# A batch's first 128 channels on all partitions for the first two steps, and half of K's weight loads moved behind V's

## The chip, the cores and the metric

The kernel runs on one core of a Trainium2 chip. The metric is device microseconds of one execution; the time before is 411.26 us, the median of three runs (411.04 to 411.67). The engines are named as in the profile: PE is the matrix engine (PEld its weight loads), ACT the scalar engine, DVE the vector engine, POOL the engine that issues the loads which convert float32 to bfloat16, SP the engine that issues the other transfers.

## What is computed

```python
# x: 8 batches x 4160 positions x 192 channels, float32; 8 heads of 24 channels, 7 taps
w = softmax(weight, axis=-1)                      # 8 x 7
y[b, t, h, g] = sum_k w[h, k] * x[b, t - 6 + k, h, g]      # causal convolution
xk = mu_k * y + (1 - mu_k) * y_prev               # y_prev: y of the position before
xr = mu_r * y + (1 - mu_r) * y_prev
k = relu(xk @ w_k)                                # 192 -> 1024
v = (k * k) @ w_v                                 # 1024 -> 192
out = sigmoid(xr @ w_r) * v                       # w_r: 192 -> 192
```

## The kernel before

Two batches are worked on as a pair, four pairs one after the other. What PE multiplies by the weights has the channels on the partitions. The 192 channels of a batch are three thirds of 64, and a plane `c` of `yT`, `xk` or `xr` holds third `c` of the pair's first batch on partitions 0 to 63 and the same third of its second batch on 64 to 127. So every product with `w_k` or `w_r` is a matmul of 64 rows, and two of them, one for each batch, run side by side in the two halves of the array (the profile shows them as `64*128`). Both halves need the weights, so `w_k` and `w_r` are loaded twice, once for partitions 0 to 63 and once for 64 to 127.

A pair is cut into steps of 512 positions; the first pair begins with one of 256. A step has slots: a slot (`k_mm`, L591) fills one PSUM tile of 128 x 1024 in six or twelve matmuls, ACT takes it out with a Relu (`k_relu`, L603), DVE squares it (`k_square`, L617). Step 0 has four slots (numbers 0 to 3), step 1 eight (4 to 11). `r` (L648) makes the gate's PSUM tile, `v_rows` (L679) multiplies the squares by `w_v`, `v_out` (L695) multiplies by the gate and sends the result out. The ring of PSUM tiles has four places, which K, the convolution, R and V share.

The order of all engines is written out by hand. `prologue` loads and prepares; `bundle_first` convolves the first two groups of positions, 3 and 4 blocks of 120 (`conv_t`, L411: matmuls of 128 rows by 32, 24, 16 or 8 columns, four at a time; `to_yT`, L421, casts the result into `yT`), and runs slots 0 to 3; `bundle_second` has slots 4 to 7, with the third group's convolution between them and a convolution in another form at its end (`conv_mm`, L391); `bundle_third` has slots 8 to 11 with R and V of step 0 between; `bundle_rest` is all the rest, and begins step 2 with slot 12. It transposes a group of convolved rows (`tr`, L500) and convolves group 4, loaded as the last thing of `prologue`, with `conv_tiles` (L317).

POOL's queue holds the converting loads in the order of `prologue`: group 1 of x, the first half of the columns of `w_k` (`load_wk`, two loads, L224), the second half (two), groups 2 and 3 of x, `w_r` (two), `w_v`, group 4 of x (four). Group 0 of x comes as float32 from the queues of ACT and SP, and ACT casts it; behind it SP loads the two rows of mixing factors (`load_mu`), which PE turns in one small matmul (`turn_mu`, L280).

Of the kernel before, what the change touches and what calls it, by code (L numbers as in the profile page):

```python
# [14 lines left out]
def kernel(  # L15
# [11 lines left out]
    nc = tc.nc  # L27
# [22 lines left out]
    SHORT = 78  # L50
    FILL = (6, 3)

    const = ctx.enter_context(tc.tile_pool(name="const", bufs=1))
# [10 lines left out]
    for p in range(NPAIR):  # L64
# [5 lines left out]
        for L in sizes:  # L70
# [3 lines left out]
            t0 += L  # L74
    T0, LAST = S - TAIL, len(steps) - 1
    NSLOT = len(slots)

# [96 lines left out]
    def load_mu(i, m):  # L174
# [3 lines left out]
        )  # L178

    place = three.tile([P, NF * STEP], FP32, tag="k2", name="x_f32")  # L180
    n = groups[0][2] * 2 * D
# [12 lines left out]
    tap8 = const.tile([8, P + 8], BF16)  # L194
    ident6 = const.tile([2 * NC, 2 * NC], FP32)
    ones6 = const.tile([2 * NC, 2 * NC], FP32)
    mu_raw = const.tile([2 * NC, P], FP32)
    warm_ps = ring.tile([P, 2, BANK], FP32, tag="k", name="warm")
# [3 lines left out]
    toe = const.tile([P, H, P], BF16)  # L202
    mu = const.tile([P, 2, NC], FP32)

# [5 lines left out]

    def load_thirds(w, m, n, cs=slice(0, NC)):
        for st in range(2):
            nc.gpsimd.dma_start(
                out=w[st * Q : (st + 1) * Q, cs, :],
                in_=bass.AP(
                    tensor=m.tensor,
                    offset=m.offset + cs.start * Q * n,
                    ap=[[n, Q], [Q * n, cs.stop - cs.start], [1, n]],
                ),
            )  # L220

    def load_wk(c0, c1):
        for st in range(2):
            nc.gpsimd.dma_start(  # L224
                out=wk[st * Q : (st + 1) * Q, :, c0:c1],
                in_=bass.AP(
                    tensor=moe_w_k.tensor,
                    offset=moe_w_k.offset + c0,
                    ap=[[DF, Q], [Q * DF, NC], [1, c1 - c0]],
                ),  # L230
            )

    def load_wr():
        load_thirds(wr, moe_w_r, D)

# [3 lines left out]
    def softmax():  # L239
        nc.vector.tensor_reduce(out=w_max, in_=w_raw, axis=mybir.AxisListType.X, op=ALU.max, negate=True)  # L240
        nc.scalar.activation(out=w_exp, in_=w_raw, func=AF.Exp, bias=w_max, accum_out=w_sum)
        nc.scalar.preload_act_table(AF.Sigmoid)
        for c in range(NC):
            cs = slice(c * Q, (c + 1) * Q)
            nc.scalar.copy(out=xbs[0][:, :, :, cs], in_=x_f32[:, :, :, cs])
# [33 lines left out]
    def turn_mu():  # L279
        nc.tensor.transpose(out=warm_ps[:, 1, 0 : 2 * NC], in_=mu_raw, identity=ident6)  # L280

# [119 lines left out]
    def conv_t(g, c, o, blocks):  # L401

        for n, i in enumerate(blocks):
            for first_piece in (True, False):
                for s in range(2):
                    for q in range(2):
                        c0 = c * Q + q * 32
                        lo, hi = c0 // G, (c0 + 31) // G
                        h, m = (hi, 32) if first_piece else (lo, hi * G - c0)
                        p0 = s * Q + q * 32  # L410
                        nc.tensor.matmul(  # L411
                            out=o[p0 : p0 + m, n * BLK : (n + 1) * BLK],
                            lhsT=xbs[g][:, i, s, c0 : c0 + m],
                            rhs=toe[:, h, 0:BLK],
                            start=True,
                            stop=True,
                        )

    def to_yT(g, c, o, b0, b1, copy):
        c0 = YC + groups[g][1] + b0 * BLK  # L420
        copy(out=yTs[0][:, c, c0 : c0 + (b1 - b0) * BLK], in_=o[:, 0 : (b1 - b0) * BLK])  # L421

# [27 lines left out]
    def new_yT(p):  # L450
        yTs[p] = two.tile([P, 3, -(-(YC + S) // 16) * 16], BF16, tag="yT", name="yT")
        y_drams[p] = dram.tile([NROW, 2 * D], BF16, tag=f"y{p % 2}", name="y_dram")
        nc.vector.memset(yTs[p][:, :, 0:YC], 0.0)

# [65 lines left out]
    def y_of(s, cs, k):  # L520

        p, t0, L, _, _ = steps[s]
        if s == LAST:
            return y_tail[:, cs, :, k : k + TAIL, :].rearrange("p c a t b -> p c a (t b)")
        return yTs[p][:, cs, YC + t0 - 1 + k : YC + t0 - 1 + k + L]

# [3 lines left out]
    def diff(s, cs=slice(0, 3)):  # L530
        L = steps[s][2]
        if cs.start == 0:
            diffs[s] = three.tile([P, 3, STEP], BF16, tag="diff", name="d")
        nc.vector.tensor_tensor(  # L534
            out=shaped(s, diffs[s][:, cs, :L]), in0=y_of(s, cs, 1), in1=y_of(s, cs, 0), op=ALU.subtract
        )

    def mix(s, i, sl=slice(0, NC)):

        L = steps[s][2]  # L540
        d = diffs[s]
        if s == 0 and i == 0:
            if sl.start == 0:
                xks[s] = two.tile([P, NC, STEP], BF16, tag="xk", name="xk")
            t = xks[s]
            c = sl.start
            nc.vector.scalar_tensor_tensor(
                out=t[:, c, :L],
                in0=d[:, c, :L],
                scalar=mu[:, i, c : c + 1],  # L550
                in1=y_of(s, sl, 0)[:, 0, :],
                op0=ALU.mult,
                op1=ALU.add,
            )
            return
        scale(s, i, *range(sl.start, sl.stop))
        add_y(s, i, sl)

    def scale(s, i, *cs):
        L = steps[s][2]  # L560
        if s not in (xks, xrs)[i]:
            (xks, xrs)[i][s] = (two, three)[i].tile([P, NC, STEP], BF16, tag=("xk", "xr")[i], name=("xk", "xr")[i])
        t = (xks, xrs)[i][s]
        for c in cs:
            nc.vector.tensor_scalar(  # L565
                out=t[:, c, :L], in0=diffs[s][:, c, :L], scalar1=mu[:, i, c : c + 1], scalar2=None, op0=ALU.mult
            )
# [7 lines left out]
    def k_mm(n, cs=range(NC)):  # L575
# [9 lines left out]

        for c in cs:
            for f in range(nf):
                fs = slice((j * nf + f) * P, (j * nf + f + 1) * P)
                for i in range(2):
                    r = slice(i * Q, (i + 1) * Q)  # L590
                    nc.tensor.matmul(  # L591
                        out=ps[:, i, f * L : (f + 1) * L],
                        lhsT=wk[r, c, fs],
                        rhs=xk[r, c, :L],
                        start=c == 0 and f == 0,
                        stop=c == NC - 1 and f == nf - 1,
                    )
# [42 lines left out]
    def r(s, j):  # L640
        xr = xrs[s]
        ps = ring.tile([P, 2, BANK], FP32, tag="k", name="ps_r")
        for k in range(2):
            ts = slice((2 * j + k) * P, (2 * j + k + 1) * P)
            for c in range(NC):
                for i in range(2):
                    q = slice(i * Q, (i + 1) * Q)
                    nc.tensor.matmul(  # L648
                        out=ps[:, i, k * D : (k + 1) * D],
                        lhsT=xr[q, c, ts],  # L650
                        rhs=wr[q, c, :],
                        start=c == 0,
# [170 lines left out]
    def prologue():  # L823
# [10 lines left out]
        load_mu(0, moe_mu_k)  # L834
        load_mu(1, moe_mu_r)
        nc.scalar.preload_act_table(AF.Exp)
        nc.vector.memset(zeros, 0.0)
# [5 lines left out]
        masks_tap()  # L843
        select_equal(ident6, 2 * NC)
        masks_band()
# [19 lines left out]
        load_wr()  # L865
        load_wv()
        x_tile(4)
        load_x(4)

    def bundle_first(ns):  # L870
        new_yT(0)
        tiles = [ring.tile([P, 2, BANK], FP32, tag="k", name="ps_t") for _ in range(2)]
        for n, (g, c) in enumerate((g, c) for g in range(2) for c in range(NC)):
            o = tiles[n % 2][:, n // 2 % 2, :]
            conv_t(g, c, o, range(groups[g][2]))
            if n == 0:
                turn_mu()
            to_yT(g, c, o, 0, groups[g][2], nc.scalar.copy)
            if g == 0:
                diff(0, slice(c, c + 1))  # L880
                if c == 0:
                    nc.vector.tensor_copy(out=mu.rearrange("p i c -> p (i c)"), in_=warm_ps[:, 1, 0 : 2 * NC])
                mix(0, 0, slice(c, c + 1))
# [16 lines left out]
    def bundle_second(b, ns):  # L900
# [7 lines left out]
        outs = [tiles[0][:, 0, :], tiles[1][:, 0, :], tiles[0][:, 1, :]]  # L908
        conv_t(g, 0, outs[0], range(4))
        to_yT(g, 0, outs[0], 0, 4, dve_)  # L910
        k_relu(ns[1])
        conv_t(g, 1, outs[1], range(4))
        to_yT(g, 1, outs[1], 0, 4, dve_)
        k_mm(ns[2])
        k_relu(ns[2])
        conv_t(g, 2, outs[2], range(4))
        to_yT(g, 2, outs[2], 0, 4, act_)
        k_mm(ns[3])
# [146 lines left out]
```

## Time and profile before

| | |
|---|---|
| runs, median | 411.26 us (411.04 to 411.67) |
| the profiled execution, span from its first to its last instruction | 409.5 us |
| its granted PE clock from 7.6 us on | 1.0 |
| PE busy | 401.2 us (98%) |
| DVE busy | 370.4 us (90%) |
| ACT busy | 354.6 us (87%) |
| K matmuls (L591), R (L648), V (L679) | 1632, 780, 4032 |
| converting loads (q0) | 16.36 MB |

The profile gives no time of its execution but the span; the median of the runs lies 1.8 us above it, and that much is taken as what lies around the span. Times in the views are microseconds from the first instruction. A row of the timeline merges neighbours of a kind: start, time until the last one's end, engine, line, operation, output and inputs, shape, count. A matmul's own time is longer than its turn: the next one starts while it still runs, so paces are taken from start to start.

### The profile page before, as it was taken

The numbers are of one execution on the slowest core, as the hardware profiler recorded it, in microseconds if no ns is written. First come the engines' busy times: TensorE is split into PE (matmuls) and PEld (weight loads), VectorE is DVE, ScalarE is ACT, GpSimd is POOL, SyncE is SP. The second block draws the span as 40 slices with busy tenths as digits, with TensorE's granted clock in tenths as the row PEclk, the third lists the DMA queues.
The fourth block names the chain that finished last, engine by engine and source line by source line (L and its number), as shares of the span: only waits on it lengthen the run. The fifth ranks groups of instructions, "written<-read, shape, count | busy, mean of one in ns | idle before, by whom it ended". The sixth has DMA issues, their size and how long they took to land.

```text
span 409.5 us, 17547 instructions
## 1 busy us (share of the span) xinstructions
PE 401.2 (98%) x7736; PEld 302.2 (74%) x7736; DVE 370.4 (90%) x672; ACT 354.6 (87%) x426; POOL 56.8 (14%) x91
## 2 busy tenths in 40 slices
PE   8899999999999999999999999999999999999996
PEld 5567777777877767777776777777777778777795
DVE  5999898988999989999999999999999899999973
ACT  6899989989888989988898998889899878877781
POOL 8622202200230202004020022000000000000000
PEclk9999999999999999999999999999999999999999
DMA  9999999997399998789995996977623856221223
GB/s 148 188 201 207 197 204 192 213 249 179 90 203 264 193 193 134 158 212 178 205 141 151 236 170 132 171 176 206 121 91 89 209 135 157 80 71 48 80 80 115
DMA packets 138955, 66.23 MB, mean 162 GB/s; under 512 B 89356, under 2 KB 138880, under 8 KB 138880
## 3 DMA queue, kind: packets, MB, share of 16 engines
q1 hardware_dynamic: 95536, 48.20, 46.9%
q0 software_dynamic: 42544, 16.36, 34.8%
q8 instruction: 60, 0.98, 0.9%
q10 hardware_dynamic: 800, 0.57, 0.5%
q14 instruction: 15, 0.12, 0.1%
HBM read 33.29 MB, written 36.86 MB: 171 GB/s over the span
## 4 chain that ended last, share of the span: by engine, by line
PE 92%; DMA 4%; POOL 1%; DVE 1%; ACT 1%; issue 1%; POOLq 0%; DVEq 0%
PE ps_v L679 41%; PE ps_k L591 39%; PE ps_r L648 8%; PE ps_c L362 2%; DMA xb<-in_x_dram 2%; DMA wk<-in_moe_w_k_dram 2%; PE ps_v L631 1%; ACT k_sb L603 1%; PE ps_c L317 0%; POOL wk L224 0%; POOL xb L152 0%; DVE k L617 0%; DVE yT L421 0%; DVE o_sb L695 0%; POOL tap L258 0%
## 5 line engine op out<-in xcount | busy, mean ns | idle before, releaser
L603 ACT ACTIVATE k_sb<-ps_k 128x1024 bf16<-128x1024 f32 x260 | 253.3, 1038 | 34.9 <-PE ps_k L591 33.8
L617 DVE TENSOR_TENSOR k<-k_sb 128x1024 bf16<-128x1024 bf16 x260 | 173.6, 688 | 26.1 <-ACT k_sb L603 25.8
L591 PE MATMUL ps_k<-xk,wk 64*128 64x512 bf16 (+1 forms) x1632 | 192.0, 367 | 1.5 <-DMA wk<-in_moe_w_k_dram 1.3
L679 PE MATMUL ps_v<-wv,k 64*128 64x192 bf16 x4032 | 188.5, 243 | 0.5 <-DMA wv<-in_moe_w_v_dram 0.5
L679 PEld LDWEIGHTS <-k 64*128 64x128 bf16 x4032 | 168.2, 94 | 13.1 <-issue 4.6
L591 PEld LDWEIGHTS <-wk 64*128 64x128 bf16 x1632 | 83.6, 94 | 56.9 <-issue 2.0
L695 DVE TENSOR_TENSOR o_sb<-ps_v,r_sb 128x768 f32<-128x768 f32 x64 | 60.9, 951 | 2.6 <-issue 2.4
L152 POOL DMA_DIRECT2D xb<-in_x_dram x62 | 43.5, 708 | 131.8 <-DVE xb L111 59.8
L659 ACT ACTIVATE r_sb<-ps_r 128x768 bf16<-128x768 f32 x65 | 53.4, 824 | 7.9 <-PE ps_v L679 5.7
L335 ACT CAST y<-ps_c 128x960 bf16<-128x960 f32 (+2 forms) x84 | 52.6, 708 | 0.0
L648 PEld LDWEIGHTS <-xr 64*128 64x128 bf16 x780 | 35.0, 94 | 14.8 <-issue 1.0
L648 PE MATMUL ps_r<-wr,xr 64*128 64x192 bf16 x780 | 43.4, 243 | 0.3 <-issue 0.3
L565 DVE TENSOR_SCALAR xr<-d,mu 128x512 bf16<-128x512 bf16 (+1 forms) x102 | 35.2, 349 | 0.0
L565 DVE TENSOR_SCALAR xk<-d,mu 128x512 bf16<-128x512 bf16 (+1 forms) x99 | 32.5, 358 | 0.1
L534 DVE TENSOR_TENSOR d<-yT 128x1536 bf16<-128x1536 bf16 (+4 forms) x36 | 31.2, 867 | 1.2 <-ACT yT L421 1.1
L571 DVE TENSOR_TENSOR xr<-xr,yT 128x1536 bf16<-128x1536 bf16 (+1 forms) x33 | 31.1, 941 | 1.1
L571 DVE TENSOR_TENSOR xk<-xk,yT 128x1536 bf16<-128x1536 bf16 (+3 forms) x33 | 30.5, 925 | 0.1
L518 POOL COPY y_tail<-yT 128x195 bf16<-128x195 bf16 x4 | 2.8, 690 | 89.1 <-DMA yT<-y_dram 89.1
L362 PEld LDWEIGHTS <-toe 32*32 32x32 bf16 x768 | 4.9, 87 | 10.2 <-issue 8.7
L362 PE MATMUL ps_c<-xb,toe 32*32 32x240 bf16 x768 | 10.7, 267 | 0.0
L125 POOL MEMSET xb<- 32x384 bf16 x3 | 1.2, 407 | 67.1 <-DVE xb L123 67.1
L411 PE MATMUL ps_t<-toe,xb 128*32 128x120 bf16 (+3 forms) x264 | 5.4, 234 | 0.3 <-ACT yT L421 0.2
(60 smaller groups left out, 61.8 us busy)
## 6 DMA issues: line engine op xcount, KB each, us to landing
out_dram<-o_sb SPq DMA_DIRECT2D x128, 192.0 KB
xb<-in_x_dram POOLq DMA_DIRECT2D x52, 240.0 KB, 8.1
y_dram<-y SPq DMA_DIRECT2D x48, 195.0 KB
y_dram<-y SPq DMA_DIRECT2D x8, 210.0 KB
xb<-in_x_dram POOLq DMA_DIRECT2D x6, 228.0 KB, 4.7
xb<-in_x_dram POOLq DMA_DIRECT2D x4, 192.0 KB, 6.5
wk<-in_moe_w_k_dram POOLq DMA_DIRECT2D x4, 192.0 KB, 6.2
wv<-in_moe_w_v_dram POOLq DMA_DIRECT2D x1, 384.0 KB, 10.1
```

The lines of the kernel that those rows point to most:

```text
L152: nc.gpsimd.dma_start(out=xb[q0 : q0 + rows, lo:hi, s, :], in_=bass.AP(tensor=x.tensor, offset=x.offset + (b * S + t0 + lo * step) * D, ap ...
L335: nc.scalar.copy(out=bass.AP(tensor=y.tensor, offset=y.offset + d, ap=[y.ap[0], [m * 2 * D, 2], [2 * D, m], [Q, 2], [1, b - a]],), in_=bas ...
L534: nc.vector.tensor_tensor(out=shaped(s, diffs[s][:, cs, :L]), in0=y_of(s, cs, 1), in1=y_of(s, cs, 0), op=ALU.subtract)
L565: nc.vector.tensor_scalar(out=t[:, c, :L], in0=diffs[s][:, c, :L], scalar1=mu[:, i, c : c + 1], scalar2=None, op0=ALU.mult)
L571: nc.vector.tensor_tensor(out=o, in0=o, in1=y_of(s, sl, 0), op=ALU.add)
L591: nc.tensor.matmul(out=ps[:, i, f * L : (f + 1) * L], lhsT=wk[r, c, fs], rhs=xk[r, c, :L], start=c == 0 and f == 0, stop=c == NC - 1 and f ...
L603: nc.scalar.activation(out=k_sb, in_=ps.rearrange("p a b -> p (a b)"), func=AF.Relu)
L617: nc.vector.tensor_tensor(out=o, in0=i, in1=i, op=ALU.mult)
L648: nc.tensor.matmul(out=ps[:, i, k * D : (k + 1) * D], lhsT=xr[q, c, ts], rhs=wr[q, c, :], start=c == 0, stop=c == NC - 1,)
L659: nc.scalar.activation(out=r_sbs[s, j], in_=r_ps.pop((s, j))[:, :, 0 : 2 * D], func=AF.Sigmoid)
L679: nc.tensor.matmul(out=v_ps[s, j][:, bank, k * D : (k + 1) * D], lhsT=k2s[s][q, f, t * P : (t + 1) * P], rhs=wv[q, f, :], start=half == 0 ...
L695: nc.vector.tensor_tensor(out=o_sb.rearrange("p (b t) d -> p b (t d)", b=2), in0=v_ps.pop((s, j)), in1=r_sbs.pop((s, j)), op=ALU.mult,)
```

## The change

For steps 0 and 1 alone (`NMIX = 2`, positions 0 to 767, `MIXED`), planes 0 and 1 are filled in another way: plane 0 holds channels 0 to 127 of the pair's first batch, plane 1 the same channels of the second batch, and plane 2 is as before (the last third of both). K and R take planes 0 and 1 with matmuls of 128 rows, in the diff's first branch (L623 for K, L689 for R in the changed kernel), and plane 2 with pairs of 64 rows (L633, L695). In every second slot plane 2 comes first.

The weights lie accordingly: plane 0 of `wk` holds rows 0 to 127 of `w_k`, plane 2 the last 64 rows twice. These are all that steps 0 and 1 need. Plane 1, which holds the first two thirds the other way round, is needed from step 2 on, and is loaded behind `w_v`; the same for `wr`.

The block of the convolution that holds position 768 is cut in two, 48 positions in the new layout and 74 in the old (positions 766 and 767 stand in both), which gives 24 matmuls more in `conv_t`, and the columns of `yT` of the first two steps move by two. The mixing factors get two more rows, loaded by two more transfers on SP. DVE scales planes 0 and 1 in one instruction where it did two (for xr of steps 0 and 1). ACT casts group 0 batch by batch.

```diff
+    def load_mu_pairs(i, m):
+        nc.sync.dma_start(
+            out=mu_raw[2 * NC + i : 2 * NC + i + 1, :],
...
     def load_wk(c0, c1):
-        for st in range(2):
-            nc.gpsimd.dma_start(out=wk[st * Q : (st + 1) * Q, :, c0:c1], ...
+        load_w(wk, moe_w_k, (0, P, 0), 0, c0, c1)
+        load_twice(wk, moe_w_k, c0, c1)
+
+    def load_rest(w, m, n):
+        for st in range(2):
+            load_w(w, m, (st * Q, (st + 1) * Q, (1 - st) * Q), 1, 0, n)
...
-        for c in cs:
+        order = [c for c in cs]
+        if s < NMIX and j % 2:
+            order = [2, 0, 1]
+        for n_c, c in enumerate(order):
             for f in range(nf):
+                if s < NMIX and c < 2:
+                    nc.tensor.matmul(
+                        out=ps[:, c, f * L : (f + 1) * L],
+                        lhsT=wk[:, 0, fs],
+                        rhs=xk[:, c, :L],
...
+                    continue
                 for i in range(2):
...
-                        lhsT=wk[r, c, fs],
+                        lhsT=wk[r, place_of(i, c), fs],
...
+                if s < NMIX and c < 2:
+                    nc.tensor.matmul(
+                        out=ps[:, c, k * D : (k + 1) * D], lhsT=xr[:, c, ts], rhs=wr[:, 0, :], start=True, stop=False
+                    )
+                    continue
...
         load_wr()
         load_wv()
+        load_rest(wk, moe_w_k, DF)
+        load_rest(wr, moe_w_r, D)
         x_tile(4)
         load_x(4)
```

POOL's queue, from the masks of `prologue` to the loads of group 4, before (a name is the tile that a load fills, and its source):

```order
L224 DMA wk<-in_moe_w_k_dram 64x3x512 x4
L152 DMA xb<-in_x_dram 128x4x192 x2
L269 AFFINE_SELECT ident<-ones_t 128x128
L152 DMA xb<-in_x_dram 128x5x192 x2
L213 DMA wr<-in_moe_w_r_dram 64x3x192 x2
L237 DMA wv<-in_moe_w_v_dram 128x8x192
```

POOL's queue at the same place, now:

```order
L225 DMA wk<-in_moe_w_k_dram 128x512
L228 DMA wk<-in_moe_w_k_dram 128x1x512
L225 DMA wk<-in_moe_w_k_dram 128x512
L228 DMA wk<-in_moe_w_k_dram 128x1x512
L154 DMA xb<-in_x_dram 128x4x192 x2
L279 AFFINE_SELECT ident<-ones_t 128x128
L154 DMA xb<-in_x_dram 128x5x192 x2
L225 DMA wr<-in_moe_w_r_dram 128x192
L228 DMA wr<-in_moe_w_r_dram 128x1x192
L248 DMA wv<-in_moe_w_v_dram 128x8x192
L225 DMA wk<-in_moe_w_k_dram 64x1024 x2
L225 DMA wr<-in_moe_w_r_dram 64x192 x2
```

The four loads of `wk` ahead of x carry two thirds of what they did, the two of `wr` likewise, and four loads with the remaining third stand between `w_v` and group 4 of x.

PE, slot 10 of step 1 between two pieces of V, before (a weight load and a matmul alternate; all are pairs of 64 rows):

```order
L679 MATMUL ps_v<-wv,k_504 128x192
L591 LDWEIGHTS wk
L591 MATMUL ps_k<-xk,wk 128x512
L591 LDWEIGHTS wk
L591 MATMUL ps_k<-xk,wk 128x512
L591 LDWEIGHTS wk
L591 MATMUL ps_k<-xk,wk 128x512
L591 LDWEIGHTS wk
L591 MATMUL ps_k<-xk,wk 128x512
```

PE at the same place, now:

```order
L726 MATMUL ps_v<-wv,k_518 128x192
L623 LDWEIGHTS wk
L623 MATMUL ps_k<-xk,wk 128x512
L623 LDWEIGHTS wk
L623 MATMUL ps_k<-xk,wk 128x512
L633 LDWEIGHTS wk
L633 MATMUL ps_k<-xk,wk 128x512
L633 LDWEIGHTS wk
L633 MATMUL ps_k<-xk,wk 128x512
L726 LDWEIGHTS k_518
L726 MATMUL ps_v<-wv,k_518 128x192
```

Two matmuls of 128 rows (L623) now stand between pieces of V and a pair of 64 rows (L633), which are all tiles of 64 rows.

More of the change, by code (lines that the diff above doesn't have):

```diff
@@ L194 @@
     tap8 = const.tile([8, P + 8], BF16)
-    ident6 = const.tile([2 * NC, 2 * NC], FP32)
-    ones6 = const.tile([2 * NC, 2 * NC], FP32)
-    mu_raw = const.tile([2 * NC, P], FP32)
+    NMU = 2 * NC + 2
+    ident6 = const.tile([NMU, NMU], FP32)
+    ones6 = const.tile([NMU, NMU], FP32)
+    mu_raw = const.tile([NMU, P], FP32)
     warm_ps = ring.tile([P, 2, BANK], FP32, tag="k", name="warm")
@@ L209, with place_of, load_w, load_twice @@
     y_tail = const.tile([P, NC, NPAIR // 2, TAIL + 1, 2], BF16)
-    def load_thirds(w, m, n, cs=slice(0, NC)):
-        for st in range(2):
[L213 to L222, printed above, removed]
-        for st in range(2):
[L224 to L231, printed above, removed]
+    def place_of(i, c):
+        return 1 - c if i and c < 2 else c
+    def load_w(w, m, rows, k, c0, c1):
+        nc.gpsimd.dma_start(out=w[rows[0] : rows[1], k, c0:c1], in_=m[rows[2] : rows[2] + rows[1] - rows[0], c0:c1])
+    def load_twice(w, m, c0, c1):
+        nc.gpsimd.dma_start(
+            out=w[:, 2, c0:c1],
+            in_=bass.AP(
+                tensor=m.tensor, offset=m.offset + P * m.shape[1] + c0, ap=[[0, 2], [m.shape[1], Q], [1, c1 - c0]]
+            ),
+        )
+    def load_wk(c0, c1):
+        load_w(wk, moe_w_k, (0, P, 0), 0, c0, c1)
+        load_twice(wk, moe_w_k, c0, c1)
+    def load_rest(w, m, n):
+        for st in range(2):
+            load_w(w, m, (st * Q, (st + 1) * Q, (1 - st) * Q), 1, 0, n)
     def load_wr():
-        load_thirds(wr, moe_w_r, D)
+        load_w(wr, moe_w_r, (0, P, 0), 0, 0, D)
+        load_twice(wr, moe_w_r, 0, D)
     def load_wv():
@@ L242, in softmax @@
         nc.scalar.preload_act_table(AF.Sigmoid)
-        for c in range(NC):
-            cs = slice(c * Q, (c + 1) * Q)
-            nc.scalar.copy(out=xbs[0][:, :, :, cs], in_=x_f32[:, :, :, cs])
+        for ss, cs in ((slice(0, 1), slice(0, P)), (slice(1, 2), slice(0, P)), (slice(0, 2), slice(P, D))):
+            nc.scalar.copy(out=xbs[0][:, :, ss, cs], in_=x_f32[:, :, ss, cs])
         nc.vector.reciprocal(out=w_sum, in_=w_sum)
@@ L279, in turn_mu @@
     def turn_mu():
-        nc.tensor.transpose(out=warm_ps[:, 1, 0 : 2 * NC], in_=mu_raw, identity=ident6)
+        nc.tensor.transpose(out=warm_ps[:, 1, 0:NMU], in_=mu_raw, identity=ident6)
     def masks_band():
@@ L401, in conv_t, with to_yT @@
     def conv_t(g, c, o, blocks):
[L403 to L421, printed above, removed]
+        pos = 0
+        for i in blocks:
+            t = groups[g][1] + i * BLK
+            if t + BLK <= MIXED:
+                parts = ((True, 0, BLK),)
+            elif t >= MIXED:
+                parts = ((False, 0, BLK),)
+            else:
+                parts = ((True, 0, MIXED - t), (False, MIXED - 2 - t, BLK))
+            for mixed, j0, j1 in parts:
+                for first_piece in (True, False):
+                    for i2 in range(2):
+                        s, ch = (c, i2) if mixed and c < 2 else (i2, c)
+                        for q in range(2):
+                            c0 = ch * Q + q * 32
+                            lo, hi = c0 // G, (c0 + 31) // G
+                            h, m = (hi, 32) if first_piece else (lo, hi * G - c0)
+                            p0 = i2 * Q + q * 32
+                            nc.tensor.matmul(
+                                out=o[p0 : p0 + m, pos : pos + j1 - j0],
+                                lhsT=xbs[g][:, i, s, c0 : c0 + m],
+                                rhs=toe[:, h, j0:j1],
+                                start=True,
+                                stop=True,
+                            )
+                pos += j1 - j0
+        return pos
+    def to_yT(g, c, o, n, copy):
+        c0 = YC + groups[g][1] - (2 if groups[g][1] < MIXED else 0)
+        copy(out=yTs[0][:, c, c0 : c0 + n], in_=o[:, 0:n])
     def conv_out(g, c, copy):
@@ L536, in diff, with mu_of @@
         )
+    def mu_of(s, i, c):
+        n = 2 * NC + i if s < NMIX and c < 2 else i * NC + c
+        return mu[:, n : n + 1]
     def mix(s, i, sl=slice(0, NC)):
@@ L563, in scale @@
         t = (xks, xrs)[i][s]
-        for c in cs:
+        runs = [(c, c + 1) for c in cs]
+        if s < NMIX and cs[:2] == (0, 1):
+            runs = [(0, 2)] + runs[2:]
+        for c, e in runs:
             nc.vector.tensor_scalar(
-                out=t[:, c, :L], in0=diffs[s][:, c, :L], scalar1=mu[:, i, c : c + 1], scalar2=None, op0=ALU.mult
+                out=t[:, c:e, :L], in0=diffs[s][:, c:e, :L], scalar1=mu_of(s, i, c), scalar2=None, op0=ALU.mult
             )
@@ L584, in k_mm @@
         nf = STEP // L
-        for c in cs:
+        order = [c for c in cs]
+        if s < NMIX and j % 2:
+            order = [2, 0, 1]
+        for n_c, c in enumerate(order):
             for f in range(nf):
                 fs = slice((j * nf + f) * P, (j * nf + f + 1) * P)
+                if s < NMIX and c < 2:
[3 more added lines that the diff above has]
+                        rhs=xk[:, c, :L],
+                        start=order[0] == 0 and f == 0,
+                        stop=order[0] == 2 and f == nf - 1,
+                    )
+                    continue
                 for i in range(2):
```

39 lines of the change are left out of this document (22 added, 17 removed).

## Prediction

> **What bounds the kernel now.** I read the busy time by stretches first, then PE's list of waits, the timelines of PE, ACT and POOL up to 30 us, and the kernel's last 15 us for prices.
>
> ```profile
> core 0: us, PE busy (x) PEld busy (x) DVE busy (x) ACT busy (x) POOL busy (x), PEclk, DMA share, GB/s
> 13.03:22.60 9.57, 8.80 (x183) 5.86 (x184) 8.66 (x18) 9.31 (x11) 5.10 (x9) 1.00 1.59 191
> ...
> 30.00:400.00 370.00, 369.49 (x7072) 279.24 (x7070) 343.45 (x610) 328.87 (x393) 38.53 (x59) 1.00 0.80 162
> ```
>
> From 30 to 400 us PE is idle for 0.5 us in 370. So the end moves by two things alone: how much earlier PE's stream arrives at 30 us, and how much longer PE itself takes for the same work behind it. In the first stretch ACT is as full as PE (9.31 of 9.57 us). PE's two longest waits in front of 30 us:
>
> ```profile
> PE ps_k L591 <- DMA wk<-in_moe_w_k_dram: 1.3, 2, 0.7
> PE ps_v L679 <- DMA wv<-in_moe_w_v_dram: 0.5, 1, 0.5
> ```
>
> Both are for weights, and the loads that end them are those that the change shortens or brings forward. PE in order of time:
>
> ```profile
> 8.21 1.86 PE L411 MATMUL ps_t<-toe,xb 128*32 128x120 bf16 x96 [0.21 <-ACT yT L421]
> 10.01 0.28 PE L591 MATMUL ps_k<-xk,wk 64*128 64x256 bf16 x1
> 10.99 1.48 PE L591 MATMUL ps_k<-xk,wk 64*128 64x256 bf16 x24 [0.70 <-DMA wk<-in_moe_w_k_dram]
> 13.03 2.78 PE L591 MATMUL ps_k<-xk,wk 64*128 64x256 bf16 x35 [0.56 <-DMA wk<-in_moe_w_k_dram]
> 15.73 1.02 PE L411 MATMUL ps_t<-toe,xb 128*32 128x120 bf16 x64
> 16.80 0.82 PE L591 MATMUL ps_k<-xk,wk 64*128 64x512 bf16 x6
> ...
> 18.74 1.52 PE L391 MATMUL ps_c<-xb,toe 64*128 64x240 bf16 x16
> 20.09 1.47 PE L591 MATMUL ps_k<-xk,wk 64*128 64x512 bf16 x12
> 21.38 0.68 PE L648 MATMUL ps_r<-wr,xr 64*128 64x192 bf16 x12
> 22.60 1.49 PE L679 MATMUL ps_v<-wv,k 64*128 64x192 bf16 x32 [0.55 <-DMA wv<-in_moe_w_v_dram]
> ...
> 26.55 1.46 PE L591 MATMUL ps_k<-xk,wk 64*128 64x512 bf16 x12
> 27.94 0.96 PE L500 MATMUL ps_t<-ident,y 120*128 120x120 bf16 x15
> 28.83 0.40 PE L317 MATMUL ps_c<-xb,toe 64*64 64x240 bf16 x8
> ```
>
> The weights' first half is there at 10.99, the second at 13.03, V's at 22.60. R's twelve matmuls would have been through at 21.38 + 0.50 = 21.88 (0.50 is their turn in the tail, below), so V's weights cost PE 0.72 us of its stream. ACT in the same time:
>
> ```profile
> 11.85 6.83 ACT L603 ACTIVATE k_sb<-ps_k 128x1024 bf16<-128x1024 f32 x7 [1.17 <-PE ps_k L591]
> 18.58 0.55 ACT L421 CAST yT<-ps_t 128x480 bf16<-128x480 f32 x1
> ...
> 21.04 1.96 ACT L603 ACTIVATE k_sb<-ps_k 128x1024 bf16<-128x1024 f32 x2
> ```
>
> Two Relus take 1.96 us, so their pace is 0.93 us, and seven without a wait take 6 x 0.93 + 1.03 = 6.61 us. Here it was 6.83: 0.22 us went to the second half of the weights. The cast that ends at 19.13 lies between PE's first and later matmuls of L391, which write beside it in the same PSUM tile. Up to there ACT sets the pace, behind it PE.
>
> **The loads.** POOL's queue, one landing from the chain of waits, and the page's row on the size of K's loads:
>
> ```profile
> 4.19 2.55 POOL L224 DMA_DIRECT2D wk<-in_moe_w_k_dram  x4
> ...
> 12.20 0.93 POOL L237 DMA_DIRECT2D wv<-in_moe_w_v_dram  x1 [0.34 <-DMA wk<-in_moe_w_k_dram]
> ...
> 22.57 0.71 POOL L152 DMA_DIRECT2D xb<-in_x_dram  x1 [1.84 <-DMA wv<-in_moe_w_v_dram]
> ```
>
> ```profile
> 18.60 8.27 DMA xb<-in_x_dram
> ```
>
> ```profile
> wk<-in_moe_w_k_dram POOLq DMA_DIRECT2D x4, 192.0 KB, 6.2
> ```
>
> - *Weights of K.* Four loads of 192 KB become four of 128 KB. PE's waits put the second landing at 10.99 and the fourth at 13.03: 1.02 us for 192 KB, so 0.34 less for each. The first half should be there at 10.99 - 0.68 = 10.3, the second at 13.03 - 1.36 = 11.7. Lower bound of the gain: none, if a load's time does not go by its size.
> - *Weights of V.* 256 KB of `wk` and 48 KB of `wr` go from before them to behind them. At the 191 GB/s of that stretch this is 1.6 us: 22.60 becomes 21.0. K's pace, 192 KB in 1.02 us, gives the same. Bounds: 22.60 (no gain) and 21.0; I take 21.0, since the loads of that stretch kept one rate.
> - *The rest of K's weights* (256 KB, 1.4 us) then lands near 22.5, and the first matmul that reads it is the one at 26.55. It is hidden by 4 us.
> - *Group 4 of x* falls behind the four new loads. No byte more stands ahead of it than before, but POOL issues four loads more at 0.64 us each, and its row at 22.57 shows that an issue can wait for a landing. Its last load lands about 26.87 (the chain's row) and is needed at 28.83: 2 us of cover. I cost it at nothing; if the cover were gone, L317 and all behind it would wait.
> - *Two loads more of mixing factors* on SP, behind all that is needed sooner. PE turns the factors here, with no wait in the row:
>
> ```profile
> 6.66 0.27 PE L280 MATMUL warm<-ident,mu_raw 6*128 6x6 f32 x1
> ```
>
> The nearest row for an issue is POOL's 0.64 each, so the delay lies between 0 and 1.3. I take 0.1, near the row that shows no wait.
>
> **The convolution.** 24 matmuls more in the stretch from 8.21. The 64 at 15.73 have a pace of 1.07 / 64 = 17 ns, so at most 0.40 us; the pieces of 48 and 74 columns together stream little more than the 120 did, so at least 0.05. I take 0.2: K can begin at 10.2 instead of 10.01, just when the weights come.
>
> **K and R as 128 rows.** The columns that stream are the same: a matmul of 128 rows takes the turn of a pair. What is new is the change of tile shape between 128 and 64 rows. Before, K, R and V had none among themselves. The kernel's last matmuls show such a change, with 64 rows ahead and 128 behind; two rows of groups give the time of a weight load there and of a transpose:
>
> ```profile
> 395.39 0.68 PE L648 MATMUL ps_r<-wr,xr 64*128 64x192 bf16 x12
> 395.89 1.50 PE L679 MATMUL ps_v<-wv,k 64*128 64x192 bf16 x32
> ...
> 399.18 1.17 PE L648 MATMUL ps_r<-wr,xr 64*128 64x192 bf16 x24
> 400.29 5.45 PE L631 MATMUL ps_v<-wv,k 128*128 128x192 bf16 x64
> ```
>
> ```profile
> L631 PEld LDWEIGHTS <-k 128*128 128x128 bf16 x64 | 5.2, 98 | 0.2 <-issue 0.2
> ```
>
> ```profile
> L500 PE MATMUL ps_t<-ident,y 120*128 120x120 bf16 x15 | 1.0, 217 | 0.0
> ```
>
> Twelve of R take 0.50 us to the next start with no change of shape behind them, so 24 would take 1.00; with the change they take 1.11. Twelve of K take 1.29 us to R (20.09 to 21.38) and 1.39 to the transposes of 120 rows (26.55 to 27.94). Back again, the last of the 15 transposes to L317: with 217 ns for the last one their pace is (0.96 - 0.22) / 14 = 53 ns, the last starts at 27.94 + 0.74 = 28.68, and L317 follows 0.15 later instead of 0.05. So a change of shape costs about 0.10 us, in both directions. I count 27 of them that were not there: 9 up to L391 (slots 0 to 7), where ACT is the bound for the most part; 6 from there to V of step 0 (three with slots 8 and 9, three inside R); 4 with slots 10 and 11; 8 with the two R of step 1. Bounds for one: 0 and 0.11; I take what the rows show.
>
> **The sum**, with minus for earlier:
> - The first Relu follows K's start by 0.86 us before (10.99 to 11.85, one matmul done ahead). Now 10.2 + 0.1 for the mixing factors + 0.86 + 0.15 for the twelfth matmul and one change of shape = 11.3: -0.55.
> - The wait inside the seven Relus goes: -0.22, of which slot 6 gives back 0.1 for its own change. At the cast at 18.58: -0.65.
> - From L391 to V six changes: +0.6. PE would be ready for V at 21.88 - 0.65 + 0.6 = 21.83, and V's weights are there. Against 22.60: -0.77.
> - Slots 10 and 11: +0.4. PE reaches slot 12 at -0.37.
> - Two R of step 1, where PE is the bound: +0.8. So +0.43 at about 37 us, and nothing behind takes it back, since PE is not idle there.
>
> DVE's two merged scalings save at most two starts and DVE isn't waited for there: 0. So the profiled span goes from 409.5 to 409.9, and the median, 1.8 above, from 411.26 to 411.7. What tells from no change is 0.2%, 0.82 us; this is inside.
>
> **A rule that speaks against it.** A matmul of 128 rows behind another of 128 rows costs here what it streams: the 64 of L631 take at most 5.45 / 64 = 85 ns each, while their weight loads last 98 ns, so the load lies beside other matmuls. The Trainium skill, "TensorE: Matmul & The Clock Gate", section "The mechanism" of part 3, says that weight loads overlap with matmuls in flight only where their row groups differ, so that full-height matmuls would not hide theirs. By that rule the 29 of the 44 new matmuls that follow their like would cost some 0.1 us more each; the row of L631 is against it.
>
> **Rivals.**
> - *Changes of shape cost nothing here*, because the next weights were loaded under way. Then -0.65 and -0.1 at L391, PE ready for V at 21.1, its weights at 21.0: -1.5 us, 409.8. For it: nothing but that K's own loads run ahead of its matmuls. Against: four places with 0.10. It would be break-even at 0.08 a change.
> - *V's weights are late as before* (slower). PE then stands at 22.60 as now, all that was won in front is lost, and 0.4 + 0.8 is added: 412.5. It decides from a landing after 21.83. For it: the issue at 12.20 waits for the fourth of the loads under way, and V's load takes ten microseconds, of which I know only the mean rate.
> - *Full-height weight loads are not hidden* (slower): eleven behind L391, +1.1, and in front each of slots 0 to 3 would take 1.05 us, more than a Relu, +0.5: 413.3.
> - *Group 4 of x is late* (slower): each microsecond after 28.4 is one lost; at 29 us 412.3.
>
> **How the numbers follow.** The forecast, a little slower inside 0.2%, has 0.59; changes that cost nothing 0.14; V's weights late 0.11; loads not hidden 0.04; group 4 late 0.05; other slips of the front of half a microsecond or more 0.07, half of them each way. In the forecast's own range (411.1 to 412.4, from 0.08 to 0.11 a change and the 0.35 between the convolution's bounds) some 0.08 lies beyond 412.08. That makes faster 0.14 + 0.035, about 0.18; slower 0.11 + 0.04 + 0.05 + 0.035 + 0.08, about 0.31; the same 0.51. The range that leaves out two in ten goes from 410.2, towards the first rival, to 412.8, past the second.
>
> **What would show it.** Right: no wait of PE for `wk` or `wv`; first Relu near 11.3; V of step 0 near 21.8; gaps of 0.1 us at each meeting of L623 or L689 with another line; each of step 1's two R 0.4 us longer than 0.5, with the changes at both its ends. Wrong: L726's first row still waiting for `wv`; R at 0.50 us as before; a wait for `xb` at L327.

## The result and the profile after

The changed kernel takes 416.01 us (median; 415.22 to 416.83) against 411.74 us of the kernel before on the same chip (411.04 to 413.82): a ratio of 1.0107, 95% interval 1.0085 to 1.0130. It is 4.3 us slower, and lies outside the predicted range (410.2 to 412.8). The profiled execution has a span of 414.5 us against 409.5. Every ratio here stands with its 95% interval and is near the quotient of the two medians, not equal to it. One execution below, of 417.31 us, was more than 1.5% above the fastest of its kernel and is left out of that kernel's ratio.

PE's list of waits of the changed kernel, first 60 us (engine, line, waited for: us, times, longest; lines left out are marked by dots):

```profile
PE ps_k L633 <- DMA wk<-in_moe_w_k_dram: 3.7, 1, 3.7
...
PE warm L290 <- DMA mu_raw<-in_moe_mu_r_dram: 0.8, 1, 0.8
...
```

V's weights are gone from the list, as predicted, but not because they came sooner (they landed at 23.01, before at 22.29): one wait for K's weights, longer than both of those before together, has taken their place. PE in order of time:

```profile
7.33 0.20 PE L290 MATMUL warm<-ident,mu_raw 8*128 8x8 f32 x1 [0.81 <-DMA mu_raw<-in_moe_mu_r_dram]
...
10.36 0.61 PE L623 MATMUL ps_k<-xk,wk 128*128 128x256 bf16 x4
14.66 0.61 PE L633 MATMUL ps_k<-xk,wk 64*128 64x256 bf16 x8 [3.69 <-DMA wk<-in_moe_w_k_dram]
...
23.55 1.53 PE L401 MATMUL ps_c<-xb,toe 64*128 64x240 bf16 x16
...
27.35 1.48 PE L726 MATMUL ps_v<-wv,k 64*128 64x192 bf16 x32
...
31.71 1.46 PE L633 MATMUL ps_k<-xk,wk 64*128 64x512 bf16 x12
...
40.48 2.11 PE L633 MATMUL ps_k<-xk,wk 64*128 64x512 bf16 x18
42.52 0.34 PE L689 MATMUL ps_r<-wr,xr 128*128 128x192 bf16 x2
42.79 0.26 PE L695 MATMUL ps_r<-wr,xr 64*128 64x192 bf16 x2
42.98 0.34 PE L689 MATMUL ps_r<-wr,xr 128*128 128x192 bf16 x2
43.25 0.26 PE L695 MATMUL ps_r<-wr,xr 64*128 64x192 bf16 x2
43.34 1.48 PE L726 MATMUL ps_v<-wv,k 64*128 64x192 bf16 x32
```

K starts at 10.36, near the forecast of 10.3, but by two errors that cancel (the points on the mixing factors and the convolution, below). Its four matmuls of 128 rows run, because the plain load of rows 0 to 127 is there; the first pair of 64 rows, which reads the third held twice, waits until 14.66. V of step 0 starts at 27.35 in place of 22.60 and slot 12 at 31.71 in place of 26.55, 5.16 us late. The chain of waits names the load, and the page's row on K's loads gives their size and the median from issue to landing (six loads of 128 KB: the four ahead of x and the two of the rest, behind `w_v`):

```profile
4.78 9.83 DMA wk<-in_moe_w_k_dram
14.61 0.05 issue
14.66 0.61 PE ps_k L633 x8
```

```profile
wk<-in_moe_w_k_dram POOLq DMA_DIRECT2D x6, 128.0 KB, 8.8
```

The load was issued at 4.78, where the second load of before stood too (4.87), and took 9.83 us. Fewer bytes (128 KB in place of 192) took longer: that second load took 6.07 us before, and the median of K's four was 6.2. The load's semaphore gets 16 events, one for each DMA engine, and they show how: 14 engines had reported by 9.25, one more at 12.89 and the last at 14.61. The reading that two engines carried its 128 rows is tried below with other counts. Stretches of the changed kernel (engines as in the first table of the prediction):

```profile
8.00:10.00 2.00, 1.51 (x120) 1.26 (x108) 1.68 (x5) 1.62 (x4) 2.00 (x4) 1.00 0.92 89
10.90:14.60 3.70, 0.07 (x1) 0.00 (x0) 2.40 (x6) 0.15 (x1) 0.18 (x1) 1.00 1.47 184
15.61:19.02 3.41, 3.41 (x20) 1.65 (x18) 2.03 (x3) 2.75 (x4) 2.64 (x5) 0.50 0.97 91
```

From 8 to 10 us, where K's weights were to come, 89 GB/s moved, against 148 in the kernel before. In the second row PE, ACT and POOL all stand. In the third, behind the idle time, the granted clock was 0.50 for 3.41 us.

### The profile page after: what moved, and what is told of

Same layout as the page of the kernel before. It is cut to its first block, busy times and chain, and to the rows that moved or that the text cites. A ratio compares the mean times of both kernels' runs of the same rounds, so it can differ in the third digit from the quotient of the medians.

```text
span 414.5 us, 17512 instructions
## 1 busy us (share of the span) xinstructions
PE 403.6 (97%) x7716; PEld 300.3 (72%) x7716; DVE 371.2 (90%) x670; ACT 354.7 (86%) x426; POOL 59.5 (14%) x95
## 4 chain that ended last, share of the span: by engine, by line
PE 95%; DMA 2%; POOL 1%; issue 0%; ACT 0%; DVE 0%; POOLq 0%; ACTq 0%
PE ps_v L726 41%; PE ps_k L633 40%; PE ps_r L695 8%; DMA wk<-in_moe_w_k_dram 2%; PE ps_c L372 2%; PE ps_k L623 2%; PE ps_v L673 1%; PE ps_c L327 0%; POOL xb L154 0%; PE ps_r L689 0%; PE ps_t L431 0%; PE ps_c L401 0%; ACT k_sb L645 0%; POOL wk L225 0%; POOL tap L268 0%
## 5 line engine op out<-in xcount | busy, mean ns | idle before, releaser
L633 PE MATMUL ps_k<-xk,wk 64*128 64x512 bf16 (+1 forms) x1568 | 187.1, 370 | 3.7 <-DMA wk<-in_moe_w_k_dram 3.7
L633 PEld LDWEIGHTS <-wk 64*128 64x128 bf16 x1568 | 80.1, 94 | 59.6 <-DMA wk<-in_moe_w_k_dram 4.0
L695 PEld LDWEIGHTS <-xr 64*128 64x128 bf16 x756 | 33.8, 94 | 14.7 <-issue 1.4
L695 PE MATMUL ps_r<-wr,xr 64*128 64x192 bf16 x756 | 42.8, 243 | 0.0
L595 DVE TENSOR_SCALAR xr<-d,mu 128x512 bf16<-128x512 bf16 (+2 forms) x100 | 35.5, 357 | 0.0
L623 PE MATMUL ps_k<-xk,wk 128*128 128x256 bf16 (+1 forms) x32 | 8.1, 377 | 0.0
```

The source lines that it names most:

```text
L595: nc.vector.tensor_scalar(out=t[:, c:e, :L], in0=diffs[s][:, c:e, :L], scalar1=mu_of(s, i, c), scalar2=None, op0=ALU.mult)
L633: nc.tensor.matmul(out=ps[:, i, f * L : (f + 1) * L], lhsT=wk[r, place_of(i, c), fs], rhs=xk[r, c, :L], start=n_c == 0 and f == 0, stop=n_ ...
L695: nc.tensor.matmul(out=ps[:, i, k * D : (k + 1) * D], lhsT=xr[q, c, ts], rhs=wr[q, place_of(i, c), :], start=c == 0, stop=c == NC - 1,)
```

## The experiments

Theory A: a load whose source pattern is `[0, 2], [row, 64]` is carried by few DMA engines, and this alone is the loss; with it mended, the prediction's sum holds. The rivals: reading the same rows twice is slow in itself; the half clock behind the wait costs as much as the wait; the loss is in the mixed tile shapes or in the other order of the loads. Each ratio is to runs of the kernel before on the same chip: at 411.74 us (23 runs) for the first four versions, at 411.39 (35) for the two with other counts and for the two with a load of x issued earlier, at 411.21 (35) for the other four.

**The repeated loads as two plain ones.**

```diff
-            nc.gpsimd.dma_start(out=w[:, 2, c0:c1], in_=bass.AP(... ap=[[0, 2], [m.shape[1], Q], [1, c1 - c0]]))
+        for st in range(2):
+            load_w(w, m, (st * Q, (st + 1) * Q, P), 2, c0, c1)
```

> The changed kernel, with the last 64 rows of w_k and w_r loaded by two loads of 64 partitions each instead of one whose source begins with a repeated dimension of two; all else as changed. Theory A (the form of that one load makes it slow: its bytes are carried by few of the DMA engines, and PE's wait of 3.7 us and the half clock behind it follow from it): no wait for K's weights above 0.3 us, the second of K's loads lands near 10.3 instead of 14.6, the granted clock stays at 1.0, and the time falls by 4 to 5 us to 411.0 to 412.2, as the sum before the result had it. Rival B (K's loads are late because the queue holds more loads and more packets, or because loads over 128 partitions are slower than over 64): the wait stays above 2 us and the time above 414. Rival C (the tile shapes cost more than 0.10 us a change): the wait goes, but the time stays above 413.

Measured: 412.48 us (410.98 to 414.92), ratio 1.0013 (0.9991 to 1.0034), not told apart from before. It reads the same 64 rows twice and has all else of the change. The wait for `wk` is gone:

```profile
...
PE warm L286 <- DMA mu_raw<-in_moe_mu_r_dram: 0.9, 1, 0.9
PE ps_t L427 <- ACT xb L251: 0.6, 1, 0.6
PE ps_k L619 <- issue: 0.3, 2, 0.2
...
```

K's six loads ahead of x landed from 8.92 to 10.67, each 3.8 to 4.7 us after its issue. So the form of the load is all of the difference from before but a rest that this run does not tell from none. Two things came otherwise than expected: the median lies 0.3 us above theory A's 412.2, and the profiled execution had a stretch at half clock after all, after PE's two waits of the list (granted clock in the sixth place behind the length):

```profile
8.68:12.09 3.41, 3.17 (x123) 2.88 (x123) 2.67 (x7) 2.15 (x5) 3.41 (x6) 0.50 1.29 155
```

**The same, with plane 2 always last.** It takes out `if s < NMIX and j % 2: order = [2, 0, 1]`.

> As the first kernel of this call, but planes always in the order 0, 1, 2, so every second slot of steps 0 and 1 meets a change of tile shape more on each side. Counted by the order of matmuls: two more changes in each pair of slots with nothing between them (slots 0 to 5 and 8 to 9: 6 + 2), none more at slots 6, 7, 10 and 11 but for where they meet V. If a change costs 0.10 us: 0.2 to 0.4 us slower than the first kernel at V of step 0 (the front is bound by ACT for a part), 0.0 to 0.5 in the whole. If a change costs nothing: the same as the first kernel within 0.1 us.

Measured: 412.22 us (411.09 to 413.41), ratio 1.0017 (1.0001 to 1.0034). The interval begins just above 1; no difference to the alternating order shows in the medians. In the traces, from the first Relu to V of step 0 it takes 11.31 us (10.69 to 22.00) in place of 10.77 (12.75 to 23.52). Its profiled execution kept the full clock, and so is the cleanest to hold against the prediction's steps (below):

```profile
6.66 0.22 PE L286 MATMUL warm<-ident,mu_raw 8*128 8x8 f32 x1
...
9.71 0.61 PE L617 MATMUL ps_k<-xk,wk 128*128 128x256 bf16 x4
...
22.00 1.48 PE L720 MATMUL ps_v<-wv,k 64*128 64x192 bf16 x32
...
26.36 1.46 PE L627 MATMUL ps_k<-xk,wk 64*128 64x512 bf16 x12
...
37.99 1.48 PE L720 MATMUL ps_v<-wv,k 64*128 64x192 bf16 x32
```

**The form of the load alone, in the kernel before.** The third plane of K's weights is loaded in the repeated form, all else is as before.

```diff
-                out=wk[st * Q : (st + 1) * Q, :, c0:c1],
+                out=wk[st * Q : (st + 1) * Q, 0:2, c0:c1],
...
+        nc.gpsimd.dma_start(out=wk[:, 2, c0:c1], in_=bass.AP(... ap=[[0, 2], [DF, Q], [1, c1 - c0]]))
```

> The kernel before, with all its tile shapes, but the last third of K's weights loaded in the form of the changed kernel (one load over 128 partitions whose source begins with a repeated dimension of two), the other two thirds by two loads of 64 partitions as before. Theory A: the third plane of slot 0 waits until about 15 us, PE's wait for K's weights is 3.5 to 5 us instead of 1.3, the clock falls to half behind it, and the kernel is 4 to 5.5 us slower than before, 415.3 to 416.8. Rival B or C: the time stays within 1 us of before.

Measured: 415.87 us (414.73 to 418.41), ratio 1.0109 (1.0077 to 1.0141). Without mixed shapes, without a weight moved behind V's, a loss of the same size is there, and so is the wait. Of the engines of the first repeated load 14 had reported by 10.36, the last two at 14.21 and 15.24:

```profile
PE ps_k L595 <- DMA wk<-in_moe_w_k_dram: 3.6, 1, 3.6
```

The rivals that put the loss on tile shapes or on the order of the loads fall.

**The clock kept up.** Eighteen matmuls that nobody reads stand ahead of slot 0 of the changed kernel, so that PE works while it would wait.

```diff
+        if n == 0:
+            for i in range(18):
+                nc.tensor.matmul(out=ps[:, i % 2, :], lhsT=ones_t, rhs=zeros, start=True, stop=True)
```

> The changed kernel with 18 matmuls of 128 x 512 on zeros put in front of slot 0, in the PSUM tile that slot 0 then overwrites: PE works through the wait for K's weights. They fill some 3.9 us. If the half clock behind the wait costs time (theory A's second part), the granted clock stays at 1.0, K and the convolution from 15.6 to 19 us run at full pace, and the time falls by 1.0 to 1.7 us against the changed kernel, to 414.3 to 415.0. If the clock costs nothing, since ACT is the bound there, the time stays within 0.4 us of the changed kernel's 416.0.

Measured: 416.45 us (415.64 to 417.25), ratio 1.0117 (1.0092 to 1.0143), no faster than the changed kernel without them (416.01, 1.0107). The clock stayed full:

```profile
7.00:30.00 23.00, 21.70 (x433) 12.43 (x428) 18.39 (x38) 16.99 (x23) 13.91 (x21) 1.00 1.31 151
```

It did so in all six runs: their mean granted clock over the span is 0.998 to 1.0, that of the changed kernel's six 0.992 to 0.996. In the two traces the half clock has a price: from the first pair of 64 rows to V of step 0 it was 11.21 us (14.19 to 25.40) in place of 12.69 (14.66 to 27.35). But of the 1.95 us that V was sooner, 0.44 were left at V's last matmul; of the rest 0.73 went into one wait for ACT, at 139.81. What the half clock costs a run on the median is thus not shown; it is not the 4.3 us.

**How many engines carry the load.** Two versions of the changed kernel, `[[0, 4], [row, 32], ...]` and `[[0, 16], [row, 8], ...]` in place of `[[0, 2], [row, 64], ...]`: the same bytes, repeated more often.

> The changed kernel, but the load of the last third reads 32 rows four times in place of 64 rows twice (so the last third of the channels is multiplied by the wrong rows in steps 0 and 1; work and bytes are the same). Theory A (a load of that form is carried by as many of the 16 DMA engines as the pattern's outermost count): four engines carry it, the load lands near 12 (between 9.3, when the other engines were through, and 14.6, half of the way), PE waits for K's weights 1 to 2 us, median 412.8 to 414. Rival B (reading the same rows again is slow in itself): it lands at 14.6 or later, 416 or more.

> The changed kernel, but the load of the last third reads 8 rows sixteen times (the last third of the channels is multiplied by the wrong rows in steps 0 and 1; work and bytes are the same). Theory A: all 16 engines carry it, it lands by 9.5, no wait of PE for K's weights, and the time is that of the kernel with halves, 411.7 to 412.8. Rival B (reading the same rows again is slow in itself): 416 or more.

Measured: 413.44 us (412.37 to 414.47), ratio 1.0045 (1.0024 to 1.0066) with four; 412.27 (411.17 to 414.22), ratio 1.0013 (0.9988 to 1.0038) with sixteen. The pages' rows on K's loads (the same six as above), four and then sixteen:

```profile
wk<-in_moe_w_k_dram POOLq DMA_DIRECT2D x6, 128.0 KB, 6.7
```

```profile
wk<-in_moe_w_k_dram POOLq DMA_DIRECT2D x6, 128.0 KB, 5.4
```

The median from issue to landing goes from 8.8 us with an outermost count of 2 to 6.7 with 4 and 5.4 with 16, and the first repeated load landed at 14.61, 11.20 and 9.84. Its semaphore shows the count itself: with 4 the last four engines reported between 10.47 and 11.20 and the other 12 by 9.21, with 16 all of them between 8.17 and 9.84. More repetition was faster, so re-reading is not the cause; the count decides. One expectation missed: with four, PE was to wait 1 to 2 us for K's weights, and the profiled execution has no such wait, since PE came to K only at 11.33. It had waited 0.71 us for the mixing factors, and its convolution was slower there (24 matmuls in 0.79 us, 0.50 in the changed kernel). The Trainium skill, "DMA: Bandwidth & Descriptors", section "Why a DMA increments its semaphore by 16 and not by 1", states the rule: the transfer is spread over the largest number up to 16 that divides the outermost count of both access patterns. With 2 on the source's side and 128 on the other that makes 2 engines, and the semaphore's events above agree.

**The rest of K's and R's weights ahead of V's**, with the plain loads: `load_rest` twice, then `load_wv`.

> The changed kernel with the repeated loads in halves, and the rest of the weights of K and R ahead of V's, as it lay before the change. Theory A (V's weights go by the bytes ahead of them, 304 KB at 191 GB/s): V's weights land 1.6 us later, about 21.9 in place of 20.3; PE is ready for V of step 0 between 22.0 and 23.5, so the wait is 0 to 0.3 us and the median 412.5 to 412.8. Rival B (the order of the queue is worth what the prediction counted, V as late as before at 22.6 or later): a wait of PE for V's weights of 0.6 us or more where it is ready at 22.0, the median 413.0 or more.

Measured: 412.80 us (411.30 to 415.15), ratio 1.0040 (1.0022 to 1.0057). V's weights landed at 22.69 where the plain loads alone had them at 20.28, and PE waited:

```profile
PE ps_v L722 <- DMA wv<-in_moe_w_v_dram: 0.3, 1, 0.3
```

The 304 KB are worth 2.4 us of landing (I had 1.6) and, where PE is ready at 22.4, a wait of 0.33 us. So this part of the change brought V's weights forward; in the medians its worth is not shown, since the interval overlaps that of the plain loads.

**Later turn of the mixing factors, R with its 128-row matmuls together, and both**, each with the plain loads. The turn stands behind the second piece of the convolution in place of the first. In R all four matmuls of 128 rows come first, then the four pairs.

```diff
-            if n == 0:
+            if n == 1:
                 turn_mu()
```

```diff
+        if s < NMIX:
+            kcs = [(k, c) for k in range(2) for c in range(2)] + [(0, 2), (1, 2)]
```

> The changed kernel with the repeated loads in halves, and PE turns the mixing factors one piece of the convolution later. Theory A (the two loads more of mixing factors hold PE up, 0.92 us in the profile of the kernel with halves, and none in that with the plain order): no wait of PE for the factors in the profile, K starts near 10, and the median is 0.2 to 0.9 us under that of the kernel with halves (412.48), so 411.6 to 412.3. Rival B (ACT's first Relu would have waited as long anyway, or DVE's mixing becomes late): K's start is then set by DVE's mixing, and the median stays within 0.2 of 412.48 or above.

> The changed kernel with the repeated loads in halves, and in R of steps 0 and 1 the four matmuls of 128 rows stand together ahead of the four pairs of 64: two changes of tile shape fewer in each of the three R. Theory A (a change costs 0.08 to 0.10 us): each R of step 1 takes 0.66 us to the next start in place of 0.82, and the median is 0.5 us under that of the kernel with halves, 412.0. Rival B (the 0.82 comes from weight loads of 128 rows that aren't hidden, 4 x 0.08): grouped they stand behind each other and R stays at 0.8 or more, no gain.

> Halves, the later turn of the mixing factors and the grouped R together. Theory A (their gains add, 0.2 to 0.9 and 0.5): 411.0 to 411.8, the same as before (411.7) or up to 0.7 us less. Rival B (the first of the two is worth nothing): 412.0.

Measured: 412.54 us (410.82 to 415.92), ratio 1.0028 (1.0002 to 1.0054), with the later turn; 411.70 (411.25 to 416.19), ratio 1.0019 (0.9997 to 1.0041), with the grouped R; 411.76 (410.30 to 412.78), ratio 1.0004 (0.9987 to 1.0021), with both. Against the 1.0013 of the plain loads none is told apart: no gain of theory A is shown in the medians. The grouped R does its part in its trace, the later turn only in one of two: alone it ran without a wait at 7.37 and K began at 10.05, but in the version with both PE still waited 0.97 us for the factors, until 7.72. R of step 1, grouped:

```profile
30.26 0.50 PE L687 MATMUL ps_r<-wr,xr 128*128 128x192 bf16 x4
30.70 0.34 PE L693 MATMUL ps_r<-wr,xr 64*128 64x192 bf16 x4
30.87 1.48 PE L724 MATMUL ps_v<-wv,k 64*128 64x192 bf16 x32
```

0.61 us to V in place of 0.82, for two changes fewer: 0.10 each. Four matmuls of 128 rows in a row take 0.44 with the change behind them, 0.34 without it, or 85 ns each; their weight loads last 98 ns (median), so these are hidden. The version with the later turn lost what it had won, in its profiled execution, to a load of x far behind the change:

```profile
61.39 0.39 PE L368 MATMUL ps_c<-xb,toe 32*32 32x240 bf16 x20 [2.33 <-DMA xb<-in_x_dram]
```

That load was issued at 48.14 and landed at 61.35; before, it was issued at 47.56, landed at 57.38 and was needed at 57.86.

**That load issued earlier**, by 3.8 us in the kernel before and by 3.4 in the version with both: `table = mix_a if g == 6` in place of `mix_c`.

> The kernel before, with the second batch of group 6 of x loaded some 3.6 us earlier (at about 42 in place of 45.5 us; it landed at 57.4, 0.5 us ahead of PE's need). Theory A (in some executions that load is late, and this makes part of the spread of 410.2 to 413.3): the highest times fall under 412.5 and the median by 0.2 to 0.6, to 410.7 to 411.0. Rival B (the spread comes from the front of the kernel): the same median, 411.2, and the same spread.

> The kernel with halves, later turn and grouped R, with the same earlier load. Theory A: no wait of PE for that load (0.78 us in the profile without it), median 411.0 to 411.4 (411.76 without it). Rival B: the same median as without it, 411.5 to 412.0.

Measured: 412.13 us (410.40 to 417.31), ratio 1.0008 (0.9988 to 1.0029), and 412.11 (411.00 to 416.34), ratio 1.0026 (0.9997 to 1.0055). Theory A falls: no gain in the medians, and the highest times are not under 412.5. In the kernel before, the load issued at 43.77 landed at 57.07, against 57.38 when issued at 47.56, so 3.8 us brought 0.3. In the version with both it landed at 56.39 in place of 58.69, and its trace has no wait for that load, where the one without the edit had 0.78 us: there theory A was right, and the median did not follow. What spreads the executions over several us stays open. No version tried beats the kernel before; the one with both is level with it.

## Why the prediction was wrong, point by point

- **The step that failed is the landing of K's weights: "The first half should be there at 10.99 - 0.68 = 10.3".** The working took a load's time by its size and the pace of before's loads. The half is complete only with the third held twice, and that landed at 14.61. The lower bound, "none, if a load's time does not go by its size", was too kind: it had no case in which a smaller load takes longer. I had costed the shape of that load (one DMA for both halves, with a repeated outermost dimension) as if it were the two loads of before. No rival had the mechanism either; the list of late loads was V's and group 4 of x. With two plain loads the first half was there at 9.35 and the second at 10.67, a microsecond sooner than worked out (10.3 and 11.7).
- **The first Relu** was to start at 11.3 and started at 15.09, nearly all of it that wait. With the plain loads and the plain order it started at 10.69; with the plain loads alone, behind PE's two waits and at half clock, at 12.75.
- **V's weights** at 21.0: with the plain loads 20.28, no wait. In the changed kernel the stalled queue put them at 23.01, and nobody waited, since PE was later still. But the working put 0.72 us of PE's stream down to them, and not all of that was theirs: in the kernel before with a load of x issued earlier they landed at 20.73, R's turn was through at 21.76, and V still began only at 22.40, against 22.60. At most 0.2 us of the 0.72 is shown to be theirs; what held V up for the rest, and why that was gone with the plain loads, stays open. So the sum's 21.83 is near the measured 22.00 in part by luck. (The issue at 12.20 waited for the third of K's loads, which landed at 11.91, not for the fourth.)
- **Mixing factors, 0.1 between 0 and 1.3:** PE waited 0.81 us in the changed kernel, 0.92 with the plain loads, nothing with the plain order. In the other profiled executions it was up to 0.97. 0.1 was too small for most, though inside the bounds. In the changed kernel it cost nothing: the wait for K's weights covers it.
- **The convolution, 0.2:** not seen. From the turn to K's start the 24 more and all others took 9.71 - 6.66 = 3.05 us with the plain order, and before K started 10.01 - 6.66 = 3.35 behind the turn. In the changed kernel it was 10.36 - 7.33 = 3.03: the turn came 0.67 later where 0.1 was forecast, the convolution took 0.32 less where 0.2 more was, and so K's start came out right.
- **Changes of shape, 0.10 each: right**, in the changed kernel itself. From L401 to V of step 0 (23.55 to 27.35) 3.80 us against 3.14 before without its wait: +0.66 for six, predicted 0.6. From V to slot 12 (27.35 to 31.71) 4.36 against 3.95: +0.41, predicted 0.4. Slots and R of step 1 (40.48 to 43.34) 2.86 against 2.44 (34.89 to 37.33 before): +0.42, predicted 0.4 for each R; the rows of before are below. The Trainium skill, "TensorEngine Tiling (Array Packing)", section "Key Properties", says that a change of tiling mode drains the engine. The rows agree that a change costs time, 0.10 us here.

```profile
34.89 2.11 PE L591 MATMUL ps_k<-xk,wk 64*128 64x512 bf16 x18
36.83 0.66 PE L648 MATMUL ps_r<-wr,xr 64*128 64x192 bf16 x12
37.33 1.48 PE L679 MATMUL ps_v<-wv,k 64*128 64x192 bf16 x32
```

- **"nothing behind takes it back": wrong by 0.85 us.** PE's 0.5 us of idle time behind 30 us, which I took as nothing, were two stalls in the profiled execution of the kernel before that the changed kernel's did not have at that place:

```profile
82.29 0.59 PE L591 MATMUL ps_k<-xk,wk 64*128 64x512 bf16 x4
83.10 0.39 PE L591 MATMUL ps_k<-xk,wk 64*128 64x512 bf16 x2 [0.22 <-issue]
83.31 1.50 PE L679 MATMUL ps_v<-wv,k 64*128 64x192 bf16 x32
...
147.23 0.59 PE L648 MATMUL ps_r<-wr,xr 64*128 64x192 bf16 x10
148.11 0.26 PE L648 MATMUL ps_r<-wr,xr 64*128 64x192 bf16 x2 [0.28 <-issue]
148.20 1.48 PE L679 MATMUL ps_v<-wv,k 64*128 64x192 bf16 x32
```

  Start to start, 1.02 us where six of K take 0.65, and 0.97 where R takes 0.49: 0.85 together. The changed kernel's V was 6.0 us behind from 37 to 75 us and 5.05 at its last matmul; these stalls are 0.85 of that, the other 0.1 has no row. The kernel before with a load of x issued earlier had the second stall and not the first, so they need not be there in every execution.
- **The rest of the sum held once the load was mended**, but for the reservation on V's weights. With the plain order V started at 22.00 (predicted 21.83), slot 12 at 26.36, -0.19 (-0.37), and V of step 1's second half at 37.99 against 37.33 before, +0.66 (+0.43). The medians with the plain loads, 1.0013 and 1.0017 of before, lie near the predicted 411.7 (1.001).
- **The rivals.** Changes that cost nothing: out, by the rows above. Full-height weight loads not hidden: out, by the grouped R. V's weights late: only with the old order of the queue, 0.33 us. Group 4 of x late: no wait for it in any profile.

## What to carry to other kernels

Cost a new DMA by its access pattern, not by its bytes: here the outermost count of the source set how many engines carried it, and a count of 2 made 128 KB slower than 192 KB had been. Where a load fills both halves of the partitions with the same rows, two plain loads were the cure here. And give a transfer that the profile does not yet contain a bound on the slow side too; "no gain" is not the worst case.

## What the runs showed of the hardware that was not expected

- The load on two engines also held up POOL's queue: its next issues waited 3.8 us for a landing (`wr` behind `wk`), and from 10.9 to 14.6 us POOL was busy for 0.18 us. The load that waited shares its semaphore with the late one, eight places ahead of it in the queue. Before the change `wv` too was issued (12.20) just behind the landing of the load eight places ahead (11.91). So a late load here delays the issue of the eighth load behind it, whatever that one carries.
- A stretch at half the granted clock lasted 3.41 us, from 15.61 to 19.02 in the changed kernel, behind 3.7 us of idle PE, and 3.41 us again, from 8.68 to 12.09 with the plain loads, where PE had only two waits of 0.6 and 0.9 us. In the profiled execution with the plain order, which had neither wait, the clock stayed full; but so it did in the version with the later turn and the grouped R, behind a wait of 0.97 us. It was 3.41 us again in the version with the later turn, behind its wait of 2.33, and 6.83 (twice that) in the kernel before with the repeated load. What wait is long enough is not shown.
- Issuing a load of x 3.8 us earlier moved its landing by 0.3 us; in another version 3.4 us moved it by 2.3.
- PE's stalls that the profile calls "issue", with nothing to wait for, have a place. The instructions come in transfers of 16 KB (queue q8), 60 in 410 us. All 11 stalls of this kind over 0.2 us behind the first of them, in 14 profiled executions, ended 1.30 to 1.53 us after one of these transfers did. The late start of V of step 0 in the kernel before (22.60) lies 1.51 us behind one, that at 22.40 lies 1.61 behind one. That the instructions' arrival is what PE waits for is likely, and no run here tests it.
